# Score sets of three PSUM banks, one exp over 1536 columns, and a two-bank ring for whole units

## Chip, cores, metric

The kernel runs on one core of one Trainium2 chip. The metric is device time in microseconds (us). The profile is one execution of the program; its span is about 2 us shorter than the measured time. A run listed as slow had a lower granted clock, which is the share of TensorE's full clock that the chip allowed it (0.752 in e4 and 0.97 in e1, against 0.973 to 1.0 in the runs that are compared); slow runs are not compared.

## The reference, cut to what matters

Two branches share one layer norm, and their outputs are added to the input.

```python
xn = layernorm(x)                                   # x: 2048 x 512, bf16
# branch A: attention, 32 heads of 16, each query sees itself and the 255 keys before it
q, k, v = split(xn @ wqkv)
p = softmax(where(0 <= i - j < 256, q @ k.T / 4, -1e9))
A = (p @ v) @ wo
# branch B: gMLP, 688 channels in each half
z1, z2 = split(gelu(xn @ w_in));  z2 = layernorm(z2)
g = w_sp @ z2 + b_sp                                # 2048 x 2048 over the tokens
B = (z1 * g) @ w_out
out = x + A + B
```

## The kernel before

Its first stage, up to about 89 us, makes the layer norm, both halves of z and most of q, k and v. The second stage is the subject. There attention works on units (J, G): J is a pair of 128-query blocks (8 of them), G a group of 8 heads (4 of them). A unit needs 12 banks of scores (a bank is a PSUM tile of 512 columns into which matmuls write): three key windows (BC, AB, CA) by four row tiles. A row tile is 32 rows of the array; it holds two heads of 16. For J = 0 half of the window falls away and 8 banks are left.

A *set* is one group of score matmuls and its exp. Here it is two banks from two row tiles:

```python
ps_s = ctx.enter_context(tc.tile_pool(name="ps_s", bufs=2, space=bass.MemoryType.PSUM))   # 2 x 2 banks
ps_o = ctx.enter_context(tc.tile_pool(name="ps_o", bufs=2, space=bass.MemoryType.PSUM))   # PV, q/k/v
ps_f = ctx.enter_context(tc.tile_pool(name="ps_f", bufs=2, space=bass.MemoryType.PSUM))   # spatial, output, q/k/v
...
def do_scores(J, G, kind, sp):
    S = ps_s.tile([P, 2, 512], F32, name="S", tag="S")
    ...
    for kb, qs, nq, col in segs:
        for i in range(2):
            s = 2 * sp + i                          # row tile
            nc.tensor.matmul(S[:, i, col : col + 2 * nq],
                lhsT=kT[32 * s : 32 * s + 32, G, kb * P : (kb + 1) * P],
                rhs=qpad[32 * s : 32 * s + 32, G, :, qs : qs + nq], start=True, stop=True)
    nc.scalar.activation(out=Et[:, 2 * sp : 2 * sp + 2, c0:512], in_=S[:, :, c0:512],
                         func=ACT.Exp, scale=SM_SCALE)
```

VectorE then multiplies the window's edges by masks. PV (the exps times v), 48 matmuls of 17 columns in a full unit, makes the output and the softmax denominators; VectorE normalises into `on`, and a transposing DMA makes `oT`. The main loop issues one set, then nine PV matmuls, then an even share of *filler*: leftover q/k/v units, spatial units (`gf`: 16 matmuls of 344 columns for each half) and output units (`fo`: 10 matmuls of 512 columns).

The softmax here doesn't subtract the row's maximum and nothing guards it: scores larger than these inputs give would overflow.

## Time and profile before

| | before |
|---|---|
| time, median of 3 at first (of 4 with the result) | 337.99 (338.1) us |
| span of the profiled run | 335.8 us |
| TensorE, ScalarE, VectorE busy | 312.3, 236.4, 195.6 us |
| score matmuls busy | 70.7 us |
| exps | 184, 184.5 us busy |

How to read it: an engine's busy share alone does not say that it is the bound; what it waits for does. TensorE hardly waits between 105 and 320 us, while ScalarE waits 38.6 us for its scores. Matmul durations include a pipelined end (0.39 us for a set that holds TensorE 0.32), so the distance from one group's start to the next one's is the cost. The lines stand in the prediction.

### The profile page before, as it was taken

Reading aid. Unit: us, or ns where it says so; the run is one execution under the profiler, and the core shown is the slowest. Engines: PE = TensorE matmul, PEld = TensorE weight load, DVE = VectorE, ACT = ScalarE, POOL = GpSimd, SP = SyncE. Lnnn points to the kernel's source line nnn. Section 1 sums busy time; section 2 is a strip of 40 time slices with the busy share of each in tenths; the row PEclk is TensorE's granted clock in tenths of the full one; section 3 lists DMA queues with packets and bytes.
Section 4 is the critical chain, followed back from the end, with each engine's and each line's share of the span. In section 5 each row is a group of like instructions: output and inputs, shape, how many; then the busy total and the mean of one; then the engine's idle time right before and its main releaser. Section 6 shows DMA issues by size and latency. Waiting matters only on the chain.

```text
span 335.8 us, 7241 instructions
## 1 busy us (share of the span) xinstructions
PE 312.3 (93%) x3079; PEld 154.9 (46%) x3104; DVE 195.6 (58%) x397; ACT 236.4 (70%) x267; POOL 34.5 (10%) x76
## 2 busy tenths in 40 slices
PE   0999999999889999999999999999999999999961
PEld 0665555555334444454445444445554454454430
DVE  5867767745657655555555565555565565565440
ACT  1566565464697888788778788878888887887800
POOL 2502001000100001010110020010000200200111
PEclk9999999999999999999999999999999999999977
DMA  7992000000000073424613341560843243421221
GB/s 266 339 226 48 0 3 0 2 0 0 2 16 3 16 127 96 86 61 92 103 49 74 83 114 17 102 120 18 134 89 75 76 61 82 101 60 25 55 64 47
DMA packets 63408, 24.61 MB, mean 73 GB/s; under 512 B 57568, under 2 KB 61840, under 8 KB 63376
## 3 DMA queue, kind: packets, MB, share of 16 engines
q1 hardware_dynamic: 61024, 18.98, 27.6%
q0 software_dynamic: 1536, 4.20, 4.1%
q10 hardware_dynamic: 816, 0.97, 0.9%
q8 instruction: 24, 0.39, 0.5%
q14 instruction: 8, 0.07, 0.1%
HBM read 8.41 MB, written 2.10 MB: 31 GB/s over the span
## 4 chain that ended last, share of the span: by engine, by line
PE 88%; DMA 3%; DVE 3%; ACT 2%; issue 2%; POOL 0%; SPq 0%; POOLq 0%; ACTq 0%
PE gf L348 23%; PE S L460 17%; PE o L503 15%; PE zp L234 11%; PE fo L374 6%; PE fo L380 4%; PE pj_f L93 4%; PE pj_o L93 4%; DMA w_in_sb<-in_B_w_in_dram 2%; PE pj_o L109 2%; PE pj_f L109 2%; DVE qpad L101 1%; ACT qpad L105 1%; DMA oT<-on_4384 1%; ACT E L467 1%
## 5 line engine op out<-in xcount | busy, mean ns | idle before, releaser
L467 ACT ACTIVATE E<-S 128x1024 bf16<-128x1024 f32 (+1 forms) x184 | 184.5, 1007 | 40.8 <-PE S L460 38.6
L348 PE MATMUL gf<-z2n,wspT 128*128 128x344 bf16 x512 | 95.2, 308 | 0.0
L460 PE MATMUL S<-qpad,kT 32*128 32x512 bf16 (+1 forms) x480 | 70.7, 329 | 2.4 <-ACT E L467 2.2
L503 PEld LDWEIGHTS <-E 128*128 128x128 bf16 x1440 | 47.7, 96 | 39.5 <-issue 32.2
L503 PE MATMUL o<-v_all,E 128*128 128x17 bf16 x1440 | 64.0, 172 | 1.7 <-DVE E L483 1.6
L483 DVE TENSOR_TENSOR E<-E,maskCA 128x2048 bf16<-128x2048 bf16 (+1 forms) x32 | 37.0, 1157 | 33.2 <-ACT E L467 33.2
L348 PEld LDWEIGHTS <-wspT 128*128 128x128 bf16 x512 | 40.7, 96 | 14.8 <-issue 1.1
L460 PEld LDWEIGHTS <-kT 32*128 32x128 bf16 x480 | 18.6, 91 | 61.0 <-issue 60.9
L234 PE MATMUL zp<-w_in_sb,xnT 128*128 128x344 bf16 x256 | 43.9, 319 | 0.3 <-DMA w_in_sb<-in_B_w_in_dram 0.3
L483 DVE TENSOR_TENSOR E<-E,maskA 128x1024 bf16<-128x1024 bf16 x32 | 22.1, 690 | 32.7 <-ACT E L467 32.7
L234 PEld LDWEIGHTS <-xnT 128*128 128x128 bf16 x256 | 25.4, 101 | 15.9 <-ACT xnT L227 0.5
L387 POOL DMA_DIRECT2D out_dram<-ot x16 | 8.7, 546 | 209.9 <-DVE ot L386 206.7
L374 PE MATMUL fo<-w_out_sb,uT 128*128 128x512 bf16 (+1 forms) x81 | 26.9, 392 | 1.0 <-issue 0.2
L354 DVE SCALAR_TENSOR_TENSOR u<-gf,b_all,z_61 128x344 bf16<-128x344 f32 x32 | 18.3, 572 | 8.8 <-PE gf L348 8.8
L386 DVE TENSOR_TENSOR ot<-fo,x_ch 128x512 bf16<-128x512 f32 x16 | 11.0, 689 | 18.4 <-PE fo L380 14.0
L105 ACT ACTIVATE qpad<-pj_o,hmask 128x512 bf16<-128x512 f32 x16 | 11.0, 689 | 15.0 <-DVE qpad L101 15.0
L483 DVE TENSOR_TENSOR E<-E,maskC 128x1024 bf16<-128x1024 bf16 x28 | 19.3, 689 | 3.8 <-ACT E L467 1.7
L101 DVE TENSOR_SCALAR qpad<-pj_o,hmask 128x512 bf16<-128x512 f32 x16 | 11.9, 743 | 15.1 <-PE pj_o L93 15.0
L380 PE MATMUL fo<-wo_sb,oT 128*128 128x512 bf16 x64 | 19.1, 379 | 0.7 <-DMA oT<-on_4384 0.7
L241 ACT ACTIVATE z_61<-zp 128x688 bf16<-128x688 f32 x16 | 12.0, 749 | 9.7 <-PE zp L234 9.4
L93 PEld LDWEIGHTS <-wqkv 128*128 128x128 bf16 x128 | 11.9, 98 | 13.6 <-issue 2.8
L197 POOL TENSOR_TENSOR rs<-ve,mhalf 128x2 f32<-128x2 f32 (+1 forms) x13 | 10.2, 786 | 75.7 <-DVE ve L194 75.7
(97 smaller groups left out, 215.2 us busy)
## 6 DMA issues: line engine op xcount, KB each, us to landing
x_ch<-in_A_x_dram POOLq DMA_DIRECT2D x16, 128.0 KB, 2.4
out_dram<-ot POOLq DMA_DIRECT2D x16, 128.0 KB, 2.0
wqkv<-in_A_wqkv_dram SPq DMA_DIRECT2D x1, 1536.0 KB, 11.4
w_in_sb<-in_B_w_in_dram ACTq DMA_DIRECT2D x1, 688.0 KB, 7.0
w_in_sb<-in_B_w_in_dram SPq DMA_DIRECT2D x1, 688.0 KB, 7.2
w_out_sb<-in_B_w_out_dram SPq DMA_DIRECT2D x1, 640.0 KB, 5.7
xt_97<-in_A_x_dram SPq DMA_DIRECT2D x1, 512.0 KB, 8.1
xt_98<-in_A_x_dram SPq DMA_DIRECT2D x1, 512.0 KB, 12.3
```

The costliest lines, as they stand in the source:

```text
L93: nc.tensor.matmul(pt[:], lhsT=wqkv[:, c, w0 : w0 + P], rhs=xnT[:, c, t0 : t0 + 512], start=(c == 0), stop=(c == NC - 1),)
L101: nc.vector.tensor_scalar(out=qpad[:, G, 0, t0 : t0 + 512], in0=pt[:], scalar1=hmask[:, 0:1], scalar2=None, op0=ALU.mult,)
L105: nc.scalar.mul(out=qpad[:, G, 1, t0 : t0 + 512], in_=pt[:], mul=hmask[:, 1:2])
L234: nc.tensor.matmul(zp[:, j, 0:HALF], lhsT=xnT[:, c, n * P : (n + 1) * P], rhs=w_in_sb[:, c, f0 : f0 + HALF], start=(c == 0), stop=(c == NC ...
L348: nc.tensor.matmul(gf[:, 0:HALF], lhsT=wspT[t][:, c, :], rhs=z2n[:, c, j * HALF : (j + 1) * HALF], start=(c == 0), stop=(c == NB - 1),)
L354: nc.vector.scalar_tensor_tensor(out=u[:, j * HALF : (j + 1) * HALF], in0=gf[:, 0:HALF], scalar=b_all[:, t : t + 1], in1=z1[:, t, j * HALF ...
L374: nc.tensor.matmul(fo[:], lhsT=uTs[t][0:K, ch, :], rhs=w_out_sb[0:K, ch, :], start=(ch == 0), stop=False,)
L380: nc.tensor.matmul(fo[:], lhsT=oTs[t][:, c, :], rhs=wo_sb[:, c, :], start=False, stop=(c == NC - 1),)
L460: nc.tensor.matmul(S[:, i, col : col + 2 * nq], lhsT=kT[32 * s : 32 * s + 32, G, kb * P : (kb + 1) * P], rhs=qpad[32 * s : 32 * s + 32, G, ...
L467: nc.scalar.activation(out=Et[:, 2 * sp : 2 * sp + 2, c0:512], in_=S[:, :, c0:512], func=ACT.Exp, scale=SM_SCALE,)
L483: nc.vector.tensor_tensor(out=ap, in0=ap, in1=m.unsqueeze(1).to_broadcast([P, ap.shape[1], ap.shape[2]]), op=ALU.mult,)
L503: nc.tensor.matmul(o[:, q, hh * VW : (hh + 1) * VW], lhsT=E[(J, G, kind)][:, s, col : col + P], rhs=v_all[:, kb, h * VW : (h + 1) * VW], s ...
```

## The change

The intent: with three banks in a set and three row tiles streaming at once, there are fewer sets, hence fewer changes between scores and other work (0.11 and 0.10 us around a set in the trace before, by the prediction's reading) and fewer fixed costs of exps (1.025 us for 1024 columns but 0.611 for 512 in the same trace). Two score buffers of three banks leave two of the eight banks that both kernels use, so PV, spatial, output and leftover q/k/v units take turns on those two (the *ring*), and each unit runs from start to end instead of being interleaved with others. A planner in the program's text orders the instructions by estimated durations: scores as soon as a buffer is free, else a unit. A finished bank must be *evacuated*, that is read by VectorE or ScalarE, before it can be written again (in the changed kernel a gf matmul waits 0.35 us for this at 146 us).

```diff
-    ps_s = ... bufs=2  # tiles of two banks
-    ps_o = ... bufs=2
-    ps_f = ... bufs=2
+    ps_s = ctx.enter_context(tc.tile_pool(name="ps_s", bufs=2, space=bass.MemoryType.PSUM))
+    ps_x = ctx.enter_context(tc.tile_pool(name="ps_x", bufs=2, space=bass.MemoryType.PSUM))
...
+            if J == 0:
+                groups = [[4, 5, 6], [7], [8, 9, 10], [11]]
+            else:
+                groups = [[0, 1, 2], [3, 4, 5], [6, 7, 8], [9, 10, 11]]
...
-        S = ps_s.tile([P, 2, 512], F32, name="S", tag="S")
+        S = ps_s.tile([P, 3, 512], F32, name="S", tag="S")
...
+        nc.scalar.activation(
+            out=E[(J, G)][:, banks[0] : banks[0] + nb, c0:512], in_=S[:, 0:nb, c0:512],
+            func=ACT.Exp, scale=SM_SCALE,
+        )
...
-            o_norm[J] = [cp.tile([P, D], BF, name=f"on{q}") for q in range(2)]
+            o_norm[J] = [cp.tile([P, D], BF, name=f"on{q}", bufs=1) for q in range(2)]
...
+        xo = cp.tile([P, D], BF, name="xo")
+        nc.gpsimd.dma_start(out=xo[:], in_=x2[t * P : (t + 1) * P, :])
...
+        nc.vector.tensor_tensor(out=xo[:], in0=fo[:], in1=xo[:], op=ALU.add)
+        nc.gpsimd.dma_start(out=out2[t * P : (t + 1) * P, :], in_=xo[:])
...
+            free = set_end[si - 2] + 0.1 if si >= 2 else 0.0
+            if free <= now and (not first or u < 3 or pv_done > u - 3):
+                end = do_scores(J, G, banks, first)
...
+        if cur is None:
+            if evac[-2] + 0.1 > now:        # the ring of two is still being read
```

More of the change, by code (lines that the diff above doesn't have):

```diff
@@ L60 @@
     w_out_sb = pers.tile([P, NFC, D], BF, name="w_out_sb")
-    xnT = pers.tile([P, NC, S_TOK], BF, name="xnT")
-    wqkv = pers.tile([P, NC, 3 * D], BF, name="wqkv")
     mhalf = pers.tile([P, 4], F32, name="mhalf")
@@ L70 @@
     warm = pers.tile([P, 8], F32, name="warm")
+    pq_ctx = ctx.enter_context(ExitStack())
+    pq = pq_ctx.enter_context(tc.tile_pool(name="pq", bufs=1, side="right"))
+    xnT = pq.tile([P, NC, S_TOK], BF, name="xnT")
+    wqkv = pq.tile([P, NC, 3 * D], BF, name="wqkv")
     wspp = ctx.enter_context(tc.tile_pool(name="wspp", bufs=2))
     sm = ctx.enter_context(tc.tile_pool(name="sm", bufs=4))
-    ps_s = ctx.enter_context(tc.tile_pool(name="ps_s", bufs=2, space=bass.MemoryType.PSUM))
-    ps_o = ctx.enter_context(tc.tile_pool(name="ps_o", bufs=2, space=bass.MemoryType.PSUM))
-    ps_f = ctx.enter_context(tc.tile_pool(name="ps_f", bufs=2, space=bass.MemoryType.PSUM))
+    psum = {}
     qkv_i = [0]
@@ L81, in bank @@
         qkv_i[0] += 1
-        if qkv_i[0] % 2:
-            return ps_o.tile([P, 512], F32, name="pj_o", tag="o")
-        return ps_f.tile([P, 512], F32, name="pj_f", tag="f")
+        if "o" in psum and qkv_i[0] % 2:
+            return psum["o"].tile([P, 512], F32, name="pj_o", tag="o")
+        return psum["f"].tile([P, 512], F32, name="pj_f", tag="f")
     def qkv_unit(b, i):
@@ L122 @@
     with ExitStack() as actx:
+        ps_s = actx.enter_context(
+            tc.tile_pool(name="psa_s", bufs=2, space=bass.MemoryType.PSUM)
+        )
+        for k in ("o", "f"):
+            psum[k] = actx.enter_context(
+                tc.tile_pool(name=f"psa_{k}", bufs=2, space=bass.MemoryType.PSUM)
+            )
         pa = actx.enter_context(tc.tile_pool(name="pa", bufs=1))
@@ L221, in transposes @@
         def transposes(n, xn):
-            tp = ps_f.tile([P, NC, P], BF, name="tp", tag="f")
+            tp = psum["f"].tile([P, NC, P], BF, name="tp", tag="f")
             for c in range(NC):
@@ L319, with late @@
         nc.vector.tensor_copy(out=b_all[:], in_=b_bf[:])
-    ep = ctx.enter_context(tc.tile_pool(name="ep", bufs=7))
-    cp = ctx.enter_context(tc.tile_pool(name="cp", bufs=2))
+    ps_s = ctx.enter_context(tc.tile_pool(name="ps_s", bufs=2, space=bass.MemoryType.PSUM))
+    ps_x = ctx.enter_context(tc.tile_pool(name="ps_x", bufs=2, space=bass.MemoryType.PSUM))
+    psum.clear()
+    psum["f"] = ps_x
+    ep = ctx.enter_context(tc.tile_pool(name="ep", bufs=3))
+    cp = ctx.enter_context(tc.tile_pool(name="cp", bufs=2))
+    late_pool = []
+    def late():
+        if not late_pool:
+            pq_ctx.close()
+            late_pool.append(
+                ctx.enter_context(tc.tile_pool(name="late", bufs=1, side="right"))
+            )
+        return late_pool[0]
     wspT = {}
@@ L332, with on_dve, on_act @@
         load_wsp(t)
+    est = {"pe": 0.0, "act": 2.0, "dve": 0.0}
+    u_ready = {}
+    o_ready = {}
+    DMA_US = 3.5
+    def on_dve(dur):
+        est["dve"] = max(est["dve"], est["pe"] + 0.15) + dur
+        return est["dve"]
+    def on_act(dur):
+        est["act"] = max(est["act"], est["pe"] + 0.15) + dur
+        return est["act"]
     uTs = {}
@@ L336 @@
     o_norm = {}
-    clock = [0]
-    u_ready = {}
-    o_ready = {}
-    DMA_STEPS = 6
-    def g_unit(t):
-        u = cp.tile([P, UPAD], BF, name="u")
-        nc.gpsimd.memset(u[:, FH:UPAD], 0.0)
-        for j in range(2):
-            gf = ps_f.tile([P, 512], F32, name="gf", tag="f")
-            for c in range(NB):
-                nc.tensor.matmul(
-                    gf[:, 0:HALF], lhsT=wspT[t][:, c, :],
-                    rhs=z2n[:, c, j * HALF : (j + 1) * HALF],
-                    start=(c == 0), stop=(c == NB - 1),
-                )
-                yield HALF
-            nc.vector.scalar_tensor_tensor(
-                out=u[:, j * HALF : (j + 1) * HALF], in0=gf[:, 0:HALF],
-                scalar=b_all[:, t : t + 1], in1=z1[:, t, j * HALF : (j + 1) * HALF],
-                op0=ALU.add, op1=ALU.mult,
-            )
-        uT = cp.tile([P, NFC, P], BF, name="uT", bufs=4)
-        nc.sync.dma_start_transpose(out=uT[:], in_=u[:])
-        uTs[t] = uT
-        u_ready[t] = clock[0] + DMA_STEPS
-        if t + 2 < NB:
-            load_wsp(t + 2)
@@ L366, with q_work, g_work @@
-    x_chs = {}
-    def f_unit(t):
-        x_ch = cp.tile([P, D], BF, name="x_ch")
-        nc.gpsimd.dma_start(out=x_ch[:], in_=x2[t * P : (t + 1) * P, :])
-        fo = ps_f.tile([P, 512], F32, name="fo", tag="f")
+    us = {}
+    def q_work(b, i):
+        for n in qkv_unit(b, i):
+            yield n / 2400.0
+        end = on_dve(0.75) if i >= 8 or i % 2 == 0 else 0.0
+        if i < 8:
+            end = max(end, on_act(0.6))
+        yield -end
+    def g_work(t, j):
+        if j == 0:
+            us[t] = cp.tile([P, UPAD], BF, name="u")
+            nc.gpsimd.memset(us[t][:, FH:UPAD], 0.0)
+        u = us[t]
+        gf = ps_x.tile([P, 512], F32, name="gf", tag="f")
+        for c in range(NB):
+            nc.tensor.matmul(
+                gf[:, 0:HALF], lhsT=wspT[t][:, c, :],
+                rhs=z2n[:, c, j * HALF : (j + 1) * HALF],
+                start=(c == 0), stop=(c == NB - 1),
+            )
+            yield HALF / 2400.0
+        nc.vector.scalar_tensor_tensor(
+            out=u[:, j * HALF : (j + 1) * HALF], in0=gf[:, 0:HALF],
+            scalar=b_all[:, t : t + 1], in1=z1[:, t, j * HALF : (j + 1) * HALF],
+            op0=ALU.add, op1=ALU.mult,
+        )
+        end = on_dve(0.6)
+        if j == 1:
+            uTs[t] = late().tile([P, NFC, P], BF, name="uT", bufs=6)
+            nc.sync.dma_start_transpose(out=uTs[t][:], in_=u[:])
+            u_ready[t] = end + DMA_US
+            if t + 2 < NB:
+                load_wsp(t + 2)
+        yield -end
@@ L372, in f_unit, with f_work @@
+    def f_work(t):
+        xo = cp.tile([P, D], BF, name="xo")
+        nc.gpsimd.dma_start(out=xo[:], in_=x2[t * P : (t + 1) * P, :])
+        fo = ps_x.tile([P, 512], F32, name="fo", tag="f")
         for ch in range(NFC):
@@ L377, in f_unit @@
             )
-            yield 512
+            yield 512 / 2400.0
         for c in range(NC):
@@ L383, in f_unit @@
             )
-            yield 512
-        ot = cp.tile([P, D], BF, name="ot")
-        nc.vector.tensor_tensor(out=ot[:], in0=fo[:], in1=x_ch[:], op=ALU.add)
-        nc.gpsimd.dma_start(out=out2[t * P : (t + 1) * P, :], in_=ot[:])
-    class Filler:
-        def __init__(self):
-            self.qkv = qkv_list
-            self.gq = list(range(NB))
-            self.fq = list(range(NB))
-            self.cur = None
-            self.credit = 0.0
-        def pick(self, drain):
-            if self.qkv:
-                return qkv_unit(*self.qkv.pop(0))
-            if self.fq:
-                t = self.fq[0]
-                if t in u_ready and t in o_ready and (
-                    drain or clock[0] >= max(u_ready[t], o_ready[t])
-                ):
-                    self.fq.pop(0)
-                    return f_unit(t)
-            if self.gq:
-                return g_unit(self.gq.pop(0))
-            return None
-        def step(self, drain=False):
-            while True:
-                if self.cur is None:
-                    self.cur = self.pick(drain)
-                    if self.cur is None:
-                        return 0
-                n = next(self.cur, 0)
-                if n:
-                    return n
-                self.cur = None
-        def pull(self, cols):
-            self.credit += cols
-            while self.credit > 0:
-                n = self.step()
-                if n == 0:
-                    self.credit = 0
-                    return
-                self.credit -= n
@@ L431 @@
-    fill = Filler()
-    sets = []
-    for J in range(NJ):
-        kinds = ["BC", "AB", "CA"] if J > 0 else ["AB", "CA"]
-        for G in range(NG):
-            for ki, kind in enumerate(kinds):
-                for sp in range(2):
-                    sets.append((J, G, kind, sp, ki == len(kinds) - 1 and sp == 1))
-    E = {}
-    def do_scores(J, G, kind, sp):
-        if sp == 0:
-            E[(J, G, kind)] = ep.tile([P, 4, 512], BF, name="E")
-        Et = E[(J, G, kind)]
-        S = ps_s.tile([P, 2, 512], F32, name="S", tag="S")
-        q0 = 2 * J * P
-        segs = {
-            "BC": [(2 * J - 1, q0, 2 * P, 0)],
-            "AB": [(2 * J, q0, 2 * P, 0)],
-            "CA": [(2 * J - 2, q0, P, 0), (2 * J + 1, q0 + P, P, 2 * P)],
-        }[kind]
-        if J == 0 and kind == "CA":
-            segs = segs[1:]
-        for kb, qs, nq, col in segs:
-            for i in range(2):
-                s = 2 * sp + i
-                nc.tensor.matmul(
-                    S[:, i, col : col + 2 * nq],
-                    lhsT=kT[32 * s : 32 * s + 32, G, kb * P : (kb + 1) * P],
-                    rhs=qpad[32 * s : 32 * s + 32, G, :, qs : qs + nq],
-                    start=True, stop=True,
-                )
-        c0 = 2 * P if (J == 0 and kind == "CA") else 0
-        nc.scalar.activation(
-            out=Et[:, 2 * sp : 2 * sp + 2, c0:512], in_=S[:, :, c0:512],
-            func=ACT.Exp, scale=SM_SCALE,
-        )
@@ L472, in do_masks @@
-    def do_masks(J, G, kind):
-        Et = E[(J, G, kind)]
-        v = Et[:].rearrange("p s (e q) -> p (s e) q", e=2)
-        if kind == "BC":
-            ap, m = v[:, :, P : 2 * P], maskC[:]
-        elif kind == "AB":
-            ap, m = v[:, :, 0:P], maskA[:]
-        elif J == 0:
-            ap, m = Et[:, :, 256:512], maskCA[:, 2:4, :].rearrange("p a q -> p (a q)")
-        else:
-            ap, m = Et[:], maskCA[:].rearrange("p a q -> p (a q)")
-        nc.vector.tensor_tensor(
-            out=ap, in0=ap,
-            in1=m.unsqueeze(1).to_broadcast([P, ap.shape[1], ap.shape[2]]), op=ALU.mult,
-        )
@@ L488, in pv_unit, with pv_work @@
-    def pv_unit(J, G):
-        o = ps_o.tile([P, 2, 8 * VW], F32, name="o", tag="o")
+            yield 512 / 2400.0
+        nc.vector.tensor_tensor(out=xo[:], in0=fo[:], in1=xo[:], op=ALU.add)
+        nc.gpsimd.dma_start(out=out2[t * P : (t + 1) * P, :], in_=xo[:])
+        yield -on_dve(0.7)
+    E = {}
+    def pv_work(J, G):
+        Et = E[(J, G)]
+        o = ps_x.tile([P, 2, 8 * VW], F32, name="o", tag="f")
         for s in range(4):
@@ L504, in pv_unit @@
                             o[:, q, hh * VW : (hh + 1) * VW],
-                            lhsT=E[(J, G, kind)][:, s, col : col + P],
+                            lhsT=Et[:, 4 * KI[kind] + s, col : col + P],
                             rhs=v_all[:, kb, h * VW : (h + 1) * VW],
@@ L508, in pv_unit @@
                         )
-                        yield 1
+                        yield 0.028
         if G == 0:
-            o_norm[J] = [cp.tile([P, D], BF, name=f"on{q}") for q in range(2)]
+            o_norm[J] = [cp.tile([P, D], BF, name=f"on{q}", bufs=1) for q in range(2)]
         ov = o[:].rearrange("p q (h w) -> p q h w", w=VW)
@@ L521, in pv_unit @@
             )
+        end = on_dve(0.85)
         if G == NG - 1:
@@ L524, in pv_unit @@
                 t = 2 * J + q
-                oTs[t] = cp.tile([P, NC, P], BF, name="oT", bufs=4)
+                oTs[t] = late().tile([P, NC, P], BF, name="oT", bufs=NB)
                 nc.sync.dma_start_transpose(out=oTs[t][:], in_=o_norm[J][q][:])
-                o_ready[t] = clock[0] + DMA_STEPS
-    pv_q = []
-    pv_cur = None
-    mask_q = []
-    PV_RATE = 9
-    total_fill = 9 * 2048 + NB * 32 * HALF + (NB - 2) * (NC + NFC) * 512
-    per_set = total_fill / len(sets)
-    i = 0
-    while i < len(sets) or mask_q or pv_q or pv_cur is not None:
-        clock[0] = i
-        if i < len(sets):
-            J, G, kind, sp, last = sets[i]
-            do_scores(J, G, kind, sp)
-        while mask_q and mask_q[0][0] <= i:
-            do_masks(*mask_q.pop(0)[1])
-        if i < len(sets):
-            if sp == 1:
-                mask_q.append((i + 1, (J, G, kind)))
-            if last:
-                pv_q.append((i + 3, (J, G)))
-        n = 0
-        while n < PV_RATE:
-            if pv_cur is None:
-                if not pv_q or pv_q[0][0] > i:
-                    break
-                pv_cur = pv_unit(*pv_q.pop(0)[1])
-            if next(pv_cur, 0):
-                n += 1
-            else:
-                pv_cur = None
-        if i < len(sets):
-            fill.pull(per_set)
-        i += 1
@@ L561 @@
-    while fill.step(True):
-        pass
+                o_ready[t] = end + DMA_US
+        yield -end
+    KI = {"BC": 0, "AB": 1, "CA": 2}
+    KN = ["BC", "AB", "CA"]
+    sets = []
+    for J in range(NJ):
+        for G in range(NG):
+            if J == 0:
+                groups = [[4, 5, 6], [7], [8, 9, 10], [11]]
+            else:
+                groups = [[0, 1, 2], [3, 4, 5], [6, 7, 8], [9, 10, 11]]
+            for k, g in enumerate(groups):
+                sets.append((J, G, g, k == 0, k == 3))
@@ new lines, in do_scores @@
+    def do_scores(J, G, banks, first):
+        if first:
+            E[(J, G)] = ep.tile([P, 12, 512], BF, name="E")
+        S = ps_s.tile([P, 3, 512], F32, name="S", tag="S")
+        q0 = 2 * J * P
+        c0 = 0
+        mms = [[], []]
+        for i, bk in enumerate(banks):
+            kind, s = KN[bk // 4], bk % 4
+            if kind == "BC":
+                segs = [(2 * J - 1, q0, 2 * P, 0)]
+            elif kind == "AB":
+                segs = [(2 * J, q0, 2 * P, 0)]
+            else:
+                segs = [(2 * J + 1, q0 + P, P, 2 * P)]
+                if J > 0:
+                    segs.append((2 * J - 2, q0, P, 0))
+                else:
+                    c0 = 2 * P
+            for k, sg in enumerate(segs):
+                mms[k].append((i, s) + sg)
+        for i, s, kb, qs, nq, col in mms[0] + mms[1]:
+            nc.tensor.matmul(
+                S[:, i, col : col + 2 * nq],
+                lhsT=kT[32 * s : 32 * s + 32, G, kb * P : (kb + 1) * P],
+                rhs=qpad[32 * s : 32 * s + 32, G, :, qs : qs + nq],
+                start=True, stop=True,
+            )
+        nb = len(banks)
+        nc.scalar.activation(
+            out=E[(J, G)][:, banks[0] : banks[0] + nb, c0:512], in_=S[:, 0:nb, c0:512],
+            func=ACT.Exp, scale=SM_SCALE,
+        )
+        est["pe"] += 0.32
+        return on_act(0.28 + nb * (512 - c0) / 1400.0)
@@ new lines, in do_mask @@
+    def do_mask(J, G, kind):
+        Et = E[(J, G)][:, 4 * KI[kind] : 4 * KI[kind] + 4, :]
+        v = Et.rearrange("p s (e q) -> p (s e) q", e=2)
+        if kind == "BC":
+            ap, m = v[:, :, P : 2 * P], maskC[:]
+        elif kind == "AB":
+            ap, m = v[:, :, 0:P], maskA[:]
+        elif J == 0:
+            ap, m = Et[:, :, 256:512], maskCA[:, 2:4, :].rearrange("p a q -> p (a q)")
+        else:
+            ap, m = Et, maskCA[:].rearrange("p a q -> p (a q)")
+        nc.vector.tensor_tensor(
+            out=ap, in0=ap,
+            in1=m.unsqueeze(1).to_broadcast([P, ap.shape[1], ap.shape[2]]), op=ALU.mult,
+        )
+        return 1.35 if ap is Et else 0.7
@@ new lines, with pick @@
+    units = [(J, G) for J in range(NJ) for G in range(NG)]
+    kinds_left = {}
+    set_end = []
+    mask_q = []
+    pv_q = []
+    pv_done = 0
+    si = 0
+    evac = [0.0, 0.0]
+    qq = list(qkv_list)
+    gq = [(t, j) for t in range(NB) for j in range(2)]
+    fq = list(range(NB))
+    f_done = 0
+    cur = None
+    def pick():
+        nonlocal f_done
+        now = est["pe"]
+        if qq:
+            return q_work(*qq.pop(0)), "q"
+        if pv_q and pv_q[0][0] <= now:
+            return pv_work(*pv_q.pop(0)[1]), "pv"
+        if fq:
+            t = fq[0]
+            ok = t in u_ready and t in o_ready and max(u_ready[t], o_ready[t]) <= now
+            gdone = NB - (len(gq) + 1) // 2
+            if ok and (gdone - t >= 3 or not gq):
+                fq.pop(0)
+                return f_work(t), "f"
+        if gq and (gq[0][1] == 1 or gq[0][0] - (NB - len(fq)) < 3):
+            return g_work(*gq.pop(0)), "g"
+        if fq and t in u_ready and t in o_ready and max(u_ready[t], o_ready[t]) <= now + 0.5:
+            fq.pop(0)
+            return f_work(t), "f"
+        return None, None
@@ new lines @@
+    kind = None
+    while si < len(sets) or mask_q or pv_q or qq or gq or fq or cur is not None:
+        now = est["pe"]
+        if si < len(sets):
+            J, G, banks, first, last = sets[si]
+            free = set_end[si - 2] + 0.1 if si >= 2 else 0.0
+            u = units.index((J, G))
+            if free <= now and (not first or u < 3 or pv_done > u - 3):
+                end = do_scores(J, G, banks, first)
+                set_end.append(end)
+                left = kinds_left.setdefault((J, G), ["BC", "AB", "CA"] if J else ["AB", "CA"])
+                while left and 4 * KI[left[0]] + 3 <= banks[-1]:
+                    mask_q.append((end + 0.1, (J, G, left.pop(0)), last and not left))
+                si += 1
+                continue
+        while mask_q and mask_q[0][0] <= now:
+            t0, m, fin = mask_q.pop(0)
+            dur = do_mask(*m)
+            est["dve"] = max(est["dve"], t0) + dur
+            if fin:
+                pv_q.append((est["dve"] + 0.2, m[:2]))
+        if cur is None:
+            if evac[-2] + 0.1 > now:
+                est["pe"] = now + 0.05
+                continue
+            cur, kind = pick()
+            if cur is None:
+                est["pe"] = now + 0.05
+                continue
+        c = next(cur)
+        if c > 0:
+            est["pe"] += c
+        else:
+            evac.append(-c)
+            est["pe"] += 0.1
+            if kind == "pv":
+                pv_done += 1
+            cur = None
```

## The prediction

> **What bounds the kernel now.** I read the page's busy table first, then its costliest groups, the chain that ended last, TensorE's own timeline in the steady stage, and the timeline of the last 10 us.
>
> ```profile
> span 335.8 us, 7241 instructions
> PE 312.3 (93%) x3079; PEld 154.9 (46%) x3104; DVE 195.6 (58%) x397; ACT 236.4 (70%) x267; POOL 34.5 (10%) x76
> PE 88%; DMA 3%; DVE 3%; ACT 2%; issue 2%; POOL 0%; SPq 0%; POOLq 0%; ACTq 0%
> ...
> L467 ACT ACTIVATE E<-S 128x1024 bf16<-128x1024 f32 (+1 forms) x184 | 184.5, 1007 | 40.8 <-PE S L460 38.6
> L348 PE MATMUL gf<-z2n,wspT 128*128 128x344 bf16 x512 | 95.2, 308 | 0.0
> L460 PE MATMUL S<-qpad,kT 32*128 32x512 bf16 (+1 forms) x480 | 70.7, 329 | 2.4 <-ACT E L467 2.2
> ...
> L503 PE MATMUL o<-v_all,E 128*128 128x17 bf16 x1440 | 64.0, 172 | 1.7 <-DVE E L483 1.6
> ```
>
> TensorE is busy 93% of the span and makes 88% of the chain. Its attention groups hardly wait (2.4 us for scores, 1.7 for PV). ScalarE is the one that waits: 38.6 us for scores. So from 105 to 320 us, where the stretch table gives TensorE 213.4 busy us of 215, only fewer TensorE microseconds can shorten the kernel. Busy matmul time is pipelined, so I take costs from start to start:
>
> ```profile
> 150.48 0.39 PE L460 MATMUL S<-qpad,kT 32*128 32x256 bf16 x4
> 150.80 0.39 PE L503 MATMUL o<-v_all,E 128*128 128x17 bf16 x9
> 151.04 0.89 PE L348 MATMUL gf<-z2n,wspT 128*128 128x344 bf16 x5
> 151.86 0.39 PE L460 MATMUL S<-qpad,kT 32*128 32x256 bf16 x4
> 152.19 0.38 PE L503 MATMUL o<-v_all,E 128*128 128x17 bf16 x9
> 152.42 0.74 PE L348 MATMUL gf<-z2n,wspT 128*128 128x344 bf16 x4
> 153.10 0.39 PE L460 MATMUL S<-qpad,kT 32*128 32x512 bf16 x2
> ```
>
> A score set holds TensorE 0.32 us before PV starts, whether it is two matmuls of 512 columns or four of 256, so the two row tiles stream at once: 512 columns[...] are 0.213 us, and 0.11 us is a handover. Nine PV matmuls take 0.24 us, 0.027 each. Five gf matmuls take 0.82 us and four 0.68, so one is about 0.145 us and about 0.10 us is lost again before the next scores. **A set thus costs 0.32 + 0.10 less rounding, 0.41 us, of which nearly half is switching.** In block row 0 the 256-column sets take 0.21 instead of 0.32, so 0.30 in all.
>
> The last 10 us show a chain of vector add, output DMA, next x load and next add, in which the load is issued behind the output on the same queue:
>
> ```profile
> 326.62 0.69 DVE L386 TENSOR_TENSOR ot<-fo,x_ch 128x512 bf16<-128x512 f32 x1 [3.41 <-PE fo L380]
> ...
> 327.60 0.55 POOL L387 DMA_DIRECT2D out_dram<-ot  x1 [6.46 <-DVE ot L386]
> 327.91 1.04 PE L380 MATMUL fo<-wo_sb,oT 128*128 128x512 bf16 x4
> 328.14 0.55 POOL L370 DMA_DIRECT2D x_ch<-in_A_x_dram  x1
> 330.67 0.69 DVE L386 TENSOR_TENSOR ot<-fo,x_ch 128x512 bf16<-128x512 f32 x1 [3.36 <-DMA x_ch<-in_A_x_dram]
> ```
>
> [...]the two losses of 0.11 and 0.10 us sit at the changes between 32-row scores and 128-row work, and none shows between PV and gf. [...]This trace has only two at once, in the time of one; three are not shown yet. [...]the by-form groups have 1025 and 611. [...]
>
> **The change part by part.** *Fewer sets.* Each of the 28 units with a full window has 12 banks: six sets become four. The four units of row 0 keep four sets each. So 184 sets become 112 + 16 = 128. If three row tiles stream in the time of two, scores fall from 176 x 0.41 + 8 x 0.30 = 74.6 us to 120 x 0.41 + 8 x 0.30 = 51.6 us: **23.0 us less TensorE time**, all on the path that sets the end.
>
> *Other TensorE work is unchanged* in amount: nine QKV units left over (36 x 0.216 = 7.8), gf 512 x 0.145 = 74.4, PV 1440 x 0.027 = 39.0, fo 160 x 0.216 = 34.5 (pitches from the same timeline). With the old scores this makes 230.3 us from the first score at 88.7 us, so 319.0; the trace ends TensorE at 328.95. The other 10 us are seen idle: about 3 in the first 10 us, 1.6 from 105 to 320, about 4 around the last PV and its transposed DMA, and a lower clock at the end (0.74). The sum closes within about a microsecond. With the new scores it is 207.3, so TensorE ends at **296.0 plus idle time**.
>
> *ScalarE.* A 1536-column exp should take 1025 + 414 (the step from 512 to 1024 columns) = 1.44 us. 112 of them are 161 us; row 0 has four times (1.44 + 0.61 + 0.82 + 0.40) = 13 us. Together 174 us against 184.5, about 10 us saved by fewer fixed costs. None of that is on the path now.
>
> *Order.* The new planner puts scores as soon as a score buffer is free, so ScalarE runs nearly full and the spatial and output units are left for the end. Its own stage needs 174 + 3 for five QKV copies + 1.3 for the table load, roughly 180 us from 90.3; TensorE has 207 to do, so some 30 us of gf and fo follow after the last exp. That removes the exposed last PV, its DMA and the clock loss, about 4.5 us that I simply leave out of the new sum.
>
> *The ring of two.* QKV, PV, gf and fo units share two banks. A unit of 1.3 (PV), 2.3 (gf half) or 2.2 us (fo) covers its predecessor's evacuation of 0.8, 0.57 or 0.69 us, unless a mask of 0.69 or 1.22 us stands ahead in VectorE's queue. I allow **3.5 us** in the middle. At the start it is worse: a q unit is evacuated by VectorE 0.75 then ScalarE 0.69 behind exps of up to 1.44, the table load occupies ScalarE until 91.6, and the second three-bank buffer lies on banks whose last QKV copy ends at 90.3. Idle of 3 us becomes an estimated **7**. TensorE then ends at 296.0 + 7 + 3.5 = 306.5.
>
> *Tail.* The gate keeps an output unit behind the third spatial unit after its own, so output units 13, 14 and 15 end the program back to back. Each x load still queues behind the previous output. Add to add is 0.29 (to the output's issue) + 0.54 + 2.53 (x issue to add start) + 0.69 = 4.05 us against 2.16 us of matmul. If unit 13's matmuls end at T, its add ends at T + 0.8, unit 15's at T + 8.9; TensorE ended at T + 4.3. So the last add is 4.6 us behind TensorE (2.4 before), plus the 4.4 us from last add to span end as before: 306.5 + 9.0 = **315.5 us span**, and about 2 more for the time measured outside the span (337.99 against 335.8): 317.
>
> **The rivals.** *Row tiles do not triple.* If the third tile is serial, a set costs 0.62 and 112 of them 69 us: only about 2 us gained, time near 336.[...] *ScalarE becomes the bound.* Then the score stage lasts 180 us or more, and any wait for scores lengthens it. The backlog still has to run after, so this gives 320 to 325. For it: ScalarE would be near 95% busy. Against: back-to-back pairs in the trace overlap (1.96 us for two of 1.02), which would cut the stage below 180. *The ring of two stalls TensorE.* At one stall of 0.2 us per unit change for 89 units it costs 18 us and leaves 330. For it: VectorE waits 67.6 us for exps with masks in front of its queue, now harmful if an evacuation stands behind. Against: the program interleaves whole units by planned evacuation ends, and planned exp and evacuation durations are close to the trace's. *A better start* than I allow would give 313.
>
> **Range and chances.** The base is well fixed (closure within a microsecond). The uncertain terms are idle at the start (3 to 9 us), stalls in the middle (1 to 12) and the tail (-2 to +1). Summed: 309 to 326, middle 317, a gain of 6%. Faster by over 2% needs under 331, which only serial row tiles or a badly stalling ring prevents: 0.94; within 2%: 0.05; slower: 0.01.
>
> **What would show it.** Right: 128 exps, the wide ones about 1.44 us; three scores to next work still 0.32 us; score busy time down by about a third; ScalarE above 85% busy to about 270 us, then none; spatial and output work alone at the end; the last adds 4 us apart. Wrong: three scores taking over 0.5 us; TensorE idle before scores (for exp) or before gf, PV and fo (for VectorE) adding to over 12 us; ScalarE idle for scores as now.

The sum: 296.0 + 7 + 3.5 + 9.0 = 315.5 us of span and about 2 outside it, put at 317. The 0.213 us for 512 columns: in the trace before, four such matmuls hold TensorE 0.86 us (77.05 to 77.91), 0.215 each. The by-form groups of 1025 and 611 are the ns of exps of 1024 and 512 columns.

## The result and the profile after

The changed kernel took **317.97 us** (316.75 to 319.3, four runs); the kernel before 338.1 in the same rounds. The ratio is 0.9411, 95% interval 0.9364 to 0.9457. Ratios here are the mean time of one kernel's fast runs over that of the other's of the same rounds, so they are not quite the ratios of the medians quoted.

The page of the changed kernel, busy table and costliest groups; its lines 519, 389, 512 and 448 answer to 467, 348, 460 and 503 of before:

```profile
span 317.6 us, 7167 instructions
PE 289.8 (91%) x3104; PEld 159.6 (50%) x3104; DVE 192.5 (61%) x397; ACT 220.0 (69%) x211; POOL 34.4 (11%) x76
...
L519 ACT ACTIVATE E<-S 128x1536 bf16<-128x1536 f32 (+3 forms) x128 | 167.8, 1372 | 11.3 <-PE S L512 9.8
L389 PE MATMUL gf<-z2n,wspT 128*128 128x344 bf16 x512 | 90.3, 316 | 0.4 <-DVE on_1882 L461 0.4
...
L512 PE MATMUL S<-qpad,kT 32*128 32x512 bf16 (+1 forms) x480 | 48.5, 333 | 3.5 <-ACT E L519 1.8
...
L448 PE MATMUL o<-v_all,E 128*128 128x17 bf16 x1440 | 46.7, 171 | 2.8 <-DVE E L537 2.3
```

TensorE is busy 22.5 us less (312.3 to 289.8), and the scores' own row falls from 70.7 to 48.5 us. The rows don't add up to the engine's time, though: PV's fell too (64.0 to 46.7) with the same matmuls, because whole units have fewer pipelined ends to count (before, nine PV matmuls were recorded as 0.39 us and held TensorE 0.24; here 15 are recorded as 0.54). That is one more reason to read starts and not busy times. ScalarE's wait for scores fell from 38.6 to 9.8 us. The chain of waits of this page is of no use: 56% of it is "issue", where nothing recorded released the engine.

The steady stage of the same run, TensorE's lines of the timeline (start, duration, engine, line, operation):

```profile
151.03 0.39 PE L512 MATMUL S<-qpad,kT 32*128 32x512 bf16 x3
151.36 0.54 PE L448 MATMUL o<-v_all,E 128*128 128x17 bf16 x15
...
152.49 0.40 PE L512 MATMUL S<-qpad,kT 32*128 32x512 bf16 x4
152.82 0.92 PE L415 MATMUL fo<-w_out_sb,uT 128*128 128x512 bf16 x3
...
154.21 0.39 PE L512 MATMUL S<-qpad,kT 32*128 32x256 bf16 x6
154.54 0.60 PE L421 MATMUL fo<-wo_sb,oT 128*128 128x512 bf16 x2
```

Three matmuls of 512 columns, or six of 256, hold TensorE 0.33 us until the next work, where two took 0.32. The third row tile is all but free.

Three places lose time. **The start**, the waits of TensorE in the timeline:

```profile
90.92 0.40 PE L512 MATMUL S<-qpad,kT 32*128 32x512 bf16 x4 [1.56 <-ACT qpad L105]
...
94.18 0.29 PE L512 MATMUL S<-qpad,kT 32*128 32x256 bf16 x3 [1.03 <-ACT E L519]
...
99.76 1.67 PE L109 MATMUL pj_f<-wqkv,xnT 128*128 128x512 bf16 x7 [0.31 <-ACT qpad L105]
```

From the first score's weight load (89.29 us) to the first gf (108.10) TensorE is busy 14.34 of 18.81 us in the stretch table, so 4.5 us are idle; in the kernel before it was 2.4 from 88.7 to 105. The first line is the first two sets (three matmuls and one), held together until the last q copy of the first stage has read its bank: the new score buffers take over that stage's PSUM. (In e7 the first sets wait 0.78 us for a v copy instead, which no score reads.)

**One stall in the middle**, the same timeline around 262 us:

```profile
260.40 0.29 DVE L461 TENSOR_TENSOR on_3987<-o,rsum 128x128 bf16<-128x128 f32 x1 [2.16 <-DMA oT<-on_3563]
...
261.80 0.29 DVE L461 TENSOR_TENSOR on_3988<-o,rsum 128x128 bf16<-128x128 f32 x1 [1.10 <-DMA oT<-on_3564]
262.01 0.68 DVE L537 TENSOR_TENSOR E<-E,maskA 128x1024 bf16<-128x1024 bf16 x1
262.61 1.22 DVE L537 TENSOR_TENSOR E<-E,maskCA 128x2048 bf16<-128x2048 bf16 x1
...
263.88 0.81 PE L448 MATMUL o<-v_all,E 128*128 128x17 bf16 x26 [2.31 <-DVE E L537]
...
266.74 2.19 PE L389 MATMUL gf<-z2n,wspT 128*128 128x344 bf16 x7
268.86 0.56 PE L512 MATMUL S<-qpad,kT 32*128 32x512 bf16 x3
```

VectorE may not overwrite the single `on` buffer before the transposing DMA of the row before has read it. Two masks stand behind it in VectorE's queue, PV waits for the masks, TensorE idles for 2.31 us, and about 2 us after that it runs at half its pace for a while: seven gf matmuls take 2.12 us to the next start, 0.30 each instead of 0.145. The granted clock between 262 and 272 us is 0.83; an estimate from the two is that about 3.4 of the 10 us ran at half clock.

**The end**, once more chained as before:

```profile
307.79 1.04 PE L421 MATMUL fo<-wo_sb,oT 128*128 128x512 bf16 x4
308.15 0.69 DVE L426 TENSOR_TENSOR xo<-fo,xo 128x512 bf16<-128x512 f32 x1 [3.33 <-DMA xo<-in_A_x_dram]
309.14 0.54 POOL L427 DMA_DIRECT2D out_dram<-xo  x1 [2.94 <-DVE xo L426]
309.67 0.55 POOL L411 DMA_DIRECT2D xo<-in_A_x_dram  x1
312.27 0.69 DVE L426 TENSOR_TENSOR xo<-fo,xo 128x512 bf16<-128x512 f32 x1 [3.42 <-DMA xo<-in_A_x_dram]
```

The adds are 4.12 us apart, and the last one ends 4.1 us after TensorE.

### The profile page after: what moved, and what is told of

Same layout as the page of the kernel before. It is cut to its first block, busy times and chain, and to the rows that moved or that the text cites. A ratio compares the mean times of both kernels' runs of the same rounds, so it can differ in the third digit from the quotient of the medians.

```text
span 317.6 us, 7167 instructions
## 1 busy us (share of the span) xinstructions
PE 289.8 (91%) x3104; PEld 159.6 (50%) x3104; DVE 192.5 (61%) x397; ACT 220.0 (69%) x211; POOL 34.4 (11%) x76
## 4 chain that ended last, share of the span: by engine, by line
issue 56%; PE 28%; POOL 5%; ACT 4%; DMA 4%; DVE 2%; POOLq 0%; SPq 0%; ACTq 0%
PE zp L241 11%; PE pj_f L93 4%; PE pj_o L93 4%; DMA w_in_sb<-in_B_w_in_dram 3%; POOL xo L411 3%; PE pj_f L109 2%; ACT E L519 2%; PE gf L389 2%; PE pj_o L109 2%; PE S L512 2%; POOL out_dram L427 1%; ACT qpad L105 1%; DVE qpad L101 1%; DMA uT<-u 1%; POOL u L385 1%
## 5 line engine op out<-in xcount | busy, mean ns | idle before, releaser
L519 ACT ACTIVATE E<-S 128x1536 bf16<-128x1536 f32 (+3 forms) x128 | 167.8, 1372 | 11.3 <-PE S L512 9.8
L389 PE MATMUL gf<-z2n,wspT 128*128 128x344 bf16 x512 | 90.3, 316 | 0.4 <-DVE on_1882 L461 0.4
L512 PE MATMUL S<-qpad,kT 32*128 32x512 bf16 (+1 forms) x480 | 48.5, 333 | 3.5 <-ACT E L519 1.8
L448 PEld LDWEIGHTS <-E 128*128 128x128 bf16 x1440 | 42.3, 96 | 15.4 <-issue 8.8
L448 PE MATMUL o<-v_all,E 128*128 128x17 bf16 x1440 | 46.7, 171 | 2.8 <-DVE E L537 2.3
L512 PEld LDWEIGHTS <-kT 32*128 32x128 bf16 x480 | 13.3, 91 | 30.6 <-issue 29.4
L426 DVE TENSOR_TENSOR xo<-fo,xo 128x512 bf16<-128x512 f32 x16 | 11.1, 691 | 28.2 <-PE fo L421 21.4
L427 POOL DMA_DIRECT2D out_dram<-xo x16 | 8.7, 545 | 172.9 <-DVE xo L426 172.9
L415 PE MATMUL fo<-w_out_sb,uT 128*128 128x512 bf16 x96 | 26.6, 381 | 0.0
L537 DVE TENSOR_TENSOR E<-E,maskC 128x1024 bf16<-128x1024 bf16 x28 | 19.2, 686 | 2.9 <-ACT E L519 2.3
L93 PE MATMUL pj_f<-xnT,wqkv 128*128 128x512 bf16 x72 | 18.2, 379 | 1.5 <-ACT xnT L234 1.3
```

The source lines that it names most:

```text
L93: nc.tensor.matmul(pt[:], lhsT=wqkv[:, c, w0 : w0 + P], rhs=xnT[:, c, t0 : t0 + 512], start=(c == 0), stop=(c == NC - 1),)
L389: nc.tensor.matmul(gf[:, 0:HALF], lhsT=wspT[t][:, c, :], rhs=z2n[:, c, j * HALF : (j + 1) * HALF], start=(c == 0), stop=(c == NB - 1),)
L415: nc.tensor.matmul(fo[:], lhsT=uTs[t][0:K, ch, :], rhs=w_out_sb[0:K, ch, :], start=(ch == 0), stop=False,)
L448: nc.tensor.matmul(o[:, q, hh * VW : (hh + 1) * VW], lhsT=Et[:, 4 * KI[kind] + s, col : col + P], rhs=v_all[:, kb, h * VW : (h + 1) * VW], ...
L512: nc.tensor.matmul(S[:, i, col : col + 2 * nq], lhsT=kT[32 * s : 32 * s + 32, G, kb * P : (kb + 1) * P], rhs=qpad[32 * s : 32 * s + 32, G, ...
L519: nc.scalar.activation(out=E[(J, G)][:, banks[0] : banks[0] + nb, c0:512], in_=S[:, 0:nb, c0:512], func=ACT.Exp, scale=SM_SCALE,)
```

## The experiments

All outputs are right. "Before" had medians of 338.2 to 339.3 us in these rounds. The edits are against the changed kernel unless said otherwise.

| run | median of the fast runs, us | ratio to before, 95% interval |
|---|---|---|
| changed kernel | 317.97 | 0.9411 (0.9364 to 0.9457) |
| e1 two-bank sets (one of four runs slow; 337.57 with it) | 337.12 | 0.9937 (0.9899 to 0.9975) |
| e2 two-bank sets, ring of four | 337.43 | 0.9946 (0.9913 to 0.9979) |
| e3 `on` doubled | 315.02 | 0.9293 (0.9246 to 0.934) |
| e4 (one of four runs slow; 315.9 with it), e10: x early | 314.64, 315.14 | 0.9316 (0.925 to 0.9382), 0.9279 (0.9249 to 0.9309) |
| e5 q/k/v first | 311.42 | 0.9212 (0.9177 to 0.9247) |
| e6 exp split | 319.99 | 0.9414 (0.9348 to 0.9481) |
| **e7 e3, e4 and e5 together** | **306.97** | **0.9079 (0.904 to 0.9118)** |
| e8 e7, scores twice | 334.73 | 0.9868 (0.9847 to 0.989) |
| e9 e7, two-bank sets | 330.19 | 0.9735 (0.971 to 0.976) |

### e1_two_bank_sets: the size of a set alone

```diff
-                groups = [[4, 5, 6], [7], [8, 9, 10], [11]]
+                groups = [[4, 5], [6, 7], [8, 9], [10, 11]]
-                groups = [[0, 1, 2], [3, 4, 5], [6, 7, 8], [9, 10, 11]]
+                groups = [[2 * k, 2 * k + 1] for k in range(6)]
```

> The changed kernel with sets of two banks again (184 sets), everything else as changed: same planner, same ring of two banks, whole units. Theory (the gain is fewer switches into and out of 32-row scores, 0.41 us of TensorE per set): 56 more sets give TensorE 23 us more, all on the path, so 318 + 23 = 341 us, about the time of the kernel before. Rival (the gain is the new order, whole units and the covered end): 320 to 327 us.

The group of score matmuls on its page:

```profile
L512 PE MATMUL S<-qpad,kT 32*128 32x512 bf16 (+1 forms) x480 | 70.3, 330 | 3.3 <-ACT E L519 1.7
```

The time goes back to 337.12 us, with the score time of before (70.3). All the rest of the change taken together is worth 0.6%; nearly the whole gain is the set's size. The difference of 19.2 us is below the expected 23 (the 19.6 in the expectation of e9 counts the slow run in). A confounder can explain it: in this run's order VectorE waited for `on` only 1.4 us in all and TensorE never stood for it, while the changed kernel did. e9 repeats the pair without that.

### e2_two_bank_sets_ring4: what the ring of two costs

```diff
 (e1, and)
-        S = ps_s.tile([P, 3, 512], F32, name="S", tag="S")
+        S = ps_s.tile([P, 2, 512], F32, name="S", tag="S")
-    ps_x = ... tc.tile_pool(name="ps_x", bufs=2, ...
+    ps_x = ... tc.tile_pool(name="ps_x", bufs=4, ...
-            if evac[-2] + 0.1 > now:
+            if evac[-4] + 0.1 > now:
```

> As the previous run, but with the PSUM of two-bank sets: two score buffers of two banks and a ring of four banks for the units, which the planner knows. Theory (whole units cover evacuation, so the ring of two costs little): within 4 us of the previous run, 337 to 341 us. Rival (the ring of two stalls TensorE by 0.2 us per unit change): 15 us or more below it.

337.43 against 337.12 us: no difference that the interval could show. This alone does not clear the ring, because e2 meets the stall of the single `on` buffer, at 123 us, and e1 does not:

```profile
123.03 0.57 DVE L461 TENSOR_TENSOR on<-o,rsum 128x128 bf16<-128x128 f32 x2 [3.42 <-DMA oT<-on]
124.79 0.76 PE L448 MATMUL o<-v_all,E 128*128 128x17 bf16 x24 [1.52 <-DVE E L537]
```

The granted clock is then 0.90 from 110 to 130 us, after 1.00 from 90 to 110. Against that, TensorE is idle for only 1.2 us between 88 and 110 us, 3.8 in e1. So a gain at the start was hidden by a loss that has nothing to do with the ring; how much of this gain is the ring's, and how much the place of the score buffers, no run separates. What clears the ring in the middle is the traces themselves. In e1, with a ring of two, TensorE is busy 163.00 of 163 us from 110 to 273 us. In the changed kernel its one recorded wait for an evacuation in these 163 us is 0.35 us at 146 us, and that evacuation itself stood behind `on`. The rival of a ring that stalls TensorE falls there: whole units of 1.3 to 2.3 us do cover their predecessor's evacuation (0.57 to 0.82 us).

### e6_split_exp: is ScalarE the bound now?

```diff
-        nc.scalar.activation(out=E[...][:, banks[0] : banks[0] + nb, ...], in_=S[:, 0:nb, c0:512], ...)
+        for a, b in ([(0, 2), (2, 3)] if nb == 3 else [(0, nb)]):
+            nc.scalar.activation(out=E[...][:, banks[0] + a : banks[0] + b, ...], in_=S[:, a:b, c0:512], ...)
-        return on_act(0.28 + nb * (512 - c0) / 1400.0)
+        return on_act(0.28 * (2 if nb == 3 else 1) + nb * (512 - c0) / 1400.0)
```

> The changed kernel with each three-bank exp issued as two (1024 and 512 columns), which the planner knows: about 0.17 us more ScalarE time for each of some 116 sets, 20 us in all. Theory (TensorE is the bound and about 30 us of spatial and output units are left behind the last exp): the last exp comes some 16 to 20 us later, the leftover shrinks, and the time rises by 0 to 5 us, to 318 to 323. Rival (ScalarE became the bound): 335 us or more.

The exps on its page, and the last PV in its timeline:

```profile
L520 ACT ACTIVATE E<-S 128x1024 bf16<-128x1024 f32 (+2 forms) x248 | 180.6, 791 | 25.3 <-PE S L512 23.2
```

```profile
302.83 1.38 PE L448 MATMUL o<-v_all,E 128*128 128x17 bf16 x48 [2.01 <-DVE E L538]
```

ScalarE's exps cost 12.8 us more (0.11 us for each of the 120 sets that were split, not the 0.17 expected: a pair takes 1.51 us, less than 1.02 + 0.61, so its halves overlap), and the last exp ends at about 301 us instead of 274. That is later than the extra work explains; ScalarE's wait for scores also rose, from 9.8 to 23.2 us, probably because the planner spaces the sets by the longer exp that it was told (not tested). The time is 319.99 us and its ratio that of the changed kernel. ScalarE is not the bound. The added time came out of the work that had been left over for the end; with none left, the last PV and its DMA are exposed again, as in the kernel before.

### e3_on_double: the stall in the middle

```diff
-            o_norm[J] = [cp.tile([P, D], BF, name=f"on{q}", bufs=1) for q in range(2)]
+            o_norm[J] = [cp.tile([P, D], BF, name=f"on{q}", bufs=2) for q in range(2)]
```

> The changed kernel with two buffers for the normalised attention output instead of one. Theory (the middle loses its time not to the ring but to that single buffer: VectorE waited 2.2 and 2.0 us for the transposing DMA of the row before with masks behind it, and TensorE then stood 2.3 us for a mask and ran at a lower clock): these waits vanish and 2 to 5 us go, 313 to 316 us. Rival (the wait only moves to the next resource): within 1 us of 318.

315.02 us, 3 us less. No wait of VectorE for `oT` is left in the trace, TensorE is busy 18.00 of 18 us from 258 to 276, and the clock there is 1.00 (15.69 busy and 0.91 in the changed kernel). e10 below, which still has the single buffer, shows the same stall again (1.97 us at 263 us, and a clock of 0.83 from 260 to 270). The stall had this cause. The clock loss came with it in both of these runs and is gone in e3; but the last section has stretches of lower clock without such a wait, so a wait alone does not explain them.

### e4_x_early and e10_x_early_again: the end

```diff
 def g_work(t, j):  # j == 0
+            xos[t] = cp.tile([P, D], BF, name="xo", bufs=5)
+            nc.gpsimd.dma_start(out=xos[t][:], in_=x2[t * P : (t + 1) * P, :])
 def f_work(t):
-        xo = cp.tile([P, D], BF, name="xo")
-        nc.gpsimd.dma_start(out=xo[:], in_=x2[t * P : (t + 1) * P, :])
+        xo = xos[t]
```

> The changed kernel with the x rows of an output unit loaded when the spatial unit of the same row begins (five buffers), so that no load stands behind an output on the queue. Theory (the last adds are 4.1 us apart because of that chain): the last add begins right after the last output matmul, the end moves forward by 3 to 4.5 us, to 313.5 to 315. Rival (the end is bound by the matmuls or by output writes, and only the wait moves): under 1.5 us.

Its profile fell into a slow execution (clock 0.752, span 361.2 us, time 363.23), so nothing is read from it. The three fast runs are 313.21, 314.64 and 317.16 us.

> The early x load once more, because its profile fell into a slow execution. Theory: the last add starts within 0.3 us of the last matmul's end, TensorE's end stays near 308 us, and the time is 313.5 to 315. Rival (the early loads gain under 2 us, as its median of 315.9 allows): 316 or more.

The last lines of the second run's timeline:

```profile
307.12 1.04 PE L423 MATMUL fo<-wo_sb,oT 128*128 128x512 bf16 x4
308.19 0.69 DVE L428 TENSOR_TENSOR xo<-fo,xo 128x512 bf16<-128x512 f32 x1 [1.68 <-PE fo L423]
```

The last add begins with the last matmul's modelled end (308.16) and waits for it alone. It starts 4.1 us earlier than in the changed kernel, of which TensorE's end gives 0.7 and the chain 3.4. Against 317.97 the medians of the fast runs fell by 3.3 and 2.8 us, about the lower edge of what was expected (3 to 4.5); the second one misses its range of 313.5 to 315 by 0.14. The ratios fell by 0.0095 and 0.0132, which is 3.2 and 4.5 us of 339. The mechanism is shown; its size is known only to about a microsecond.

### e5_qkv_first: the start

```diff
-        r = z_stats(NB - 1)
-        z_apply(NB - 2, r)
-        z_apply(NB - 1, r)
+        for k in range(9):          # [remark added here] all leftover q/k/v units, with the four banks of stage one
+            if k == 4:
+                r = z_stats(NB - 1)
+            if k == 6:
+                z_apply(NB - 2, r)
+                z_apply(NB - 1, r)
+            for _ in qkv_unit(*qkv_list.pop(0)):
+                pass
```

> The changed kernel with the nine leftover QKV units issued before the first scores, while the four alternating banks of the first stage still exist. Theory (about 5 us of TensorE are idle at the start because QKV units share two banks whose ScalarE copies queue with exps, and the clock drops after it; ScalarE has slack to start later): the start loses at most 2 us, the time falls by 3 to 6 us, to 312 to 315. Rival (ScalarE starting 7 us later is not free, or the idle time moves to the first masks): 318 or more.

311.42 us, 6.5 us less: above the expected range. Two things came together. From 90 to 110 us TensorE is busy 19.02 us, against 16.18 in the changed kernel. And the shifted order happened to miss the `on` stall: TensorE's longest wait for a mask is 0.2 us here. So part of e3's gain is counted in it.

### e7_all_three: a version that beats both

The edits of e3, e4 and e5 together.

> The three mends together: double buffer, early x, QKV first. Theory (three separate places on one TensorE path): the gains add up, 318 - 3.5 - 3.7 - 4.5 = 306 us, 304 to 309. Rival (they recover the same idle time): no better than the best one alone, 313.

306.97 us (306.87 to 307.21). The gains nearly add: 3.0 (e3) + 3.1 (mean of e4 and e10) + 6.5 (e5) would give 305.4; the overlap of e3 and e5 is the likely rest. Its page:

```profile
span 305.3 us, 7136 instructions
PE 285.3 (93%) x3081; PEld 159.5 (52%) x3104; DVE 192.3 (63%) x397; ACT 220.3 (72%) x211; POOL 34.5 (11%) x76
...
PE 88%; DVE 3%; DMA 3%; ACT 2%; issue 2%; POOL 0%; SPq 0%; POOLq 0%
```

TensorE makes 88% of the chain again. What is left is its work.

### e9_two_bank_mended: the price of a set, without the stalls

The `groups` edit of e1, on e7.

> The kernel with the three mends, with sets of two banks again (184 sets instead of 128). Theory (0.41 us of TensorE for each set, free of the waits on the single buffer that clouded the first such pair): 23 us more, 329 to 331 us. Rival (0.35 us or less, as the first pair of medians reads, 19.6 us for 56 sets): 324 to 327 us.

330.19 against 306.97 us: 23.2 us for 56 sets, 0.41 us each. In both traces TensorE has no wait above 0.2 us after the first set. The 0.34 of the first pair (19.2 us) was low because one of its two kernels carried the stall: with the 3 us of e3 it comes to 22.2.

### e8_scores_twice: streaming or switching?

```diff
 (on e7)
-        for i, s, kb, qs, nq, col in mms[0] + mms[1]:
+        for i, s, kb, qs, nq, col in mms[0] + mms[0] + mms[1] + mms[1]:
-        est["pe"] += 0.32
+        est["pe"] += 0.53
```

> The kernel with the three mends, with every score matmul issued twice inside its set (same result; the planner knows), so that streaming doubles and the number of switches stays. Theory (of the 0.41 us of a set 0.21 is streaming, shared by its row tiles, and 0.20 is switching): 120 sets by 0.213 and 8 by 0.107 make 26 us more, 307 + 26 = 333 us, and scores to next work is 0.53 us. Rival (the whole 0.41 us belongs to the matmuls and their weight loads): it doubles, 307 + 50 = 357 us.

TensorE's timeline in the steady stage:

```profile
150.02 0.61 PE L519 MATMUL S<-qpad,kT 32*128 32x512 bf16 x6
150.56 0.52 PE L455 MATMUL o<-v_all,E 128*128 128x17 bf16 x14
...
152.99 0.61 PE L519 MATMUL S<-qpad,kT 32*128 32x256 bf16 x12
153.53 1.05 PE L397 MATMUL gf<-z2n,wspT 128*128 128x344 bf16 x6
```

334.73 us, 27.8 more (26 expected, 50 for the rival), and the hold is 0.54 us. Some 1.4 us of the 27.8 are a lower clock, by an estimate from the means of the profiled runs (0.993 over 332.8 us, 0.997 over 305.3 in e7). Twice the streaming adds 0.21 us to a set, so the other 0.20 us of its 0.41 does not depend on the matmuls in it. By its place in the timeline, after the last score matmul and before the first, it is paid for leaving and re-entering the 128-row work (the two losses of 0.11 and 0.10 us that the prediction read there in the trace before).

## Why the prediction was right, point by point

- **The bound** (TensorE, from 105 to 320 us): right. Adding 12.8 us to ScalarE (e6) changed nothing in the ratio; adding TensorE time (e8, e9) came through in full.
- **0.41 us per set, 23.0 us for 56 sets**: right in size and in its split. e9 measured 23.2 us, e8 the half that streams. The third row tile streams beside the other two, 0.33 us against 0.32. The 0.213 us taken for 512 columns came out as 0.21 in e8.
- **The exp of 1.44 us**: 1.451 by form in the trace, 1.385 apart in a run of eleven (15.30 us for all: 15.30 - 1.45, divided by 10). So the exps took 167.8 us, not 174. The last one ended at 274 us, not "about 270".
- **The ring of two, 3.5 us in the middle**: right in size, wrong in cause, and this is the step that failed. The traces show the ring to cost 0.35 us in the middle of the changed kernel and nothing in that of e1. The middle lost time to a part of the diff that the prediction never costed, the single `on` buffer, and to the clock drop after the stall: 3 us by e3. The two errors offset each other, so that the size fits is luck.
- **7 us of idle at the start**: over-sized. 4.5 us are idle. The first 1.6 of them are the predicted wait for the first stage's last q copy, though for both first sets and not only the second buffer's. In the profiled run a lower clock (0.88 and 0.78 in the next two stretches of 5 us) brought it near 6.2; e3's trace, with the same start, has the full clock there, so this does not belong to every run.
- **The tail**: right. Adds 4.12 us apart (4.05 predicted), the last ending 4.1 us after TensorE (4.6), and 4.6 us more to the end (4.4). e10 takes the chain away.
- **The exposed end of before, 4.5 us, left out**: right. In the changed kernel about 35 us of work, one PV unit and for the rest spatial and output units, followed the last exp (some 30 predicted); e6, which uses it up, gets the exposure back.
- **Sum**: TensorE ended at 308.8 us in the profile (306.5), the span was 317.6 (315.5), and that profiled execution was the slowest of four; the median is 317.97 against 317. Two sums are off without bearing on this: the range's own terms give 308.5 to 328.5, not 309 to 326, and the rival of serial row tiles leaves out the 16 sets of block row 0 (about 7 us at its own costs); with them it gains nothing.

Why a rearrangement with so many parts gained no more than the sets did: in e1, which has all of them but the larger sets, they gain 0.6% together. Covering the end and making units whole bought little more than the idle start and the chained tail cost, and the changed kernel then paid some 3 us for the single buffer. The parts that gain were not tested one by one. e7 is what is left when those costs go.

## What to carry to other kernels

Where TensorE alternates between row-tiled and full-array work, count the changes, not the matmuls: here a change and its return cost 0.20 us and further row tiles in the same visit cost 0.01. When a buffer count is cut to make room, cost every cut count, also the ones far from the bound: a single buffer behind a DMA reached TensorE through VectorE's queue, and half the pace came after it (gf matmuls at 0.30 instead of 0.145 us). A gain that equals its main term may hide losses of its own; look for them in the start and the end of the trace.

## What the traces add, and what stays open

- Going into 32-row scores and back costs TensorE 0.20 us here (e8). The hold of TensorE until the next work is 0.32 us for two row tiles, and 0.33 for three and for four (two sets back to back in the first row of the changed kernel, 90.92 to 91.25 us).
- The clock fell after gaps of 2.31 us (changed kernel: gf matmuls at 0.30 instead of 0.145 us, granted clock 0.83 from 262 to 272 us) and of 1.97 us (e10: 0.83 from 260 to 270), and without the gap (e3) it stayed at 1.00 there. Nor is such a gap needed: the clock was 0.92 from 110 to 130 us in e1, where TensorE was busy 20.00 of the 20 us and where, after the 1.6 us before the first set, no recorded wait of its matmuls was above 0.6 us. It was 0.88 and 0.78 from 105 to 115 us in the changed kernel after a wait of 0.46 us, while e3 with the same wait kept 1.00. What decides it stays open here.
- In the changed kernel a DMA releases a buffer whose writer sits in VectorE's queue ahead of unrelated masks (VectorE waited 2.16 us for it at 260 us). This transposing DMA landed in 2.4 to 2.6 us in 11 of 16 cases, but took 4.6 and 4.7 us just before the stall.
